# Expert 0's late half, first layer: upper weights against x's two parts side by side

## The chip, the cores and the metric

The kernel runs on one core of one Trainium2 chip. The metric is device time in microseconds (us) of one execution. The kernel before takes 385.37 us (median of 3 runs, 385.09 to 385.86).

## What is computed

A retention layer over 4 sequences of 768 tokens and 8 heads gives 3072 tokens x of 512 features. A gate picks one expert of 8 for each token, and the token's result is the expert's two-layer network, weighted by the gate. Cut to what matters here:

```python
logits = x @ w_gate
expert_idx = np.argmax(logits, axis=1)
...
for e in range(E):
    xe = x[expert_idx == e]
    h = np.maximum(xe @ w1[e], 0.0)      # 512 -> 1024, the first layer
    ye = h @ w2[e]                       # 1024 -> 512, the second layer
    out[expert_idx == e] = gate_w[expert_idx == e, None] * ye
```

The matmuls run on numbers that are rounded to a shorter form (fp32r). To keep fp32's precision, each operand is split into an upper part (the rounded number) and a lower part (what the rounding left), and each product is made of three: upper weights times upper x, lower weights times upper x, upper weights times lower x.

## The kernel before, in words

The retention layer comes first, in 24 chunks of 128 tokens; its rows are scattered by expert into a buffer in HBM. Expert 0's tokens are in two halves: an early one of 192 tokens, whose network runs while the last chunks are still being sent (`early_half`, lines 793 to 841), and a late one of 224 tokens, with which `moe_main` (line 845) begins. The other seven experts follow, at 380 to 452 tokens each.

In `moe_main` the order of the work on each engine is the order of the program, written out by hand (`manual_schedule`, line 986); the framework adds the waits that the data ask for. One pass of the loop over e (line 987) is one expert. Its first layer is a loop over eight blocks f of 128 hidden features (line 1033). For each f:

- TensorE (PE): 12 matmuls into one of three PSUM tiles `ph` (line 1035, taken in turn), 4 blocks of 128 input features for each of the three products (lines 1037 to 1043). The tile must be free: what was read from it three blocks ago must have been read. For expert 0 they have 224 columns.
- ScalarE (ACT): ReLU of `ph` into the upper part `hh` (line 1053). For expert 0 this is two instructions, of 64 and 160 columns, since 64 of the late tokens are put beside the early half's rows.
- VectorE (DVE): the lower part `hl`, ReLU of `ph` minus `hh` (line 1055), for expert 0 again two instructions.
- behind these, on the same queues, the jobs that the program hangs at this f (lines 996 to 1031): for expert 0 at f = 1 two memsets of columns 392 to 451 of `ph0` and `ph1`, at f = 2 a memset of the tile `rare` of the second layer, four small instructions of `token_index` and a memset of the same columns of `ph2`, at f = 3 and f = 4 a part each of the splitting of expert 1's weights (a cast on ACT, line 171, then a subtraction on DVE, line 173), at f = 7 the making of expert 1's x (transposes on DVE, casts on ACT, subtractions on DVE and GpSimd) and two more parts of the splitting. The memsets give columns that a later expert's shorter matmuls leave alone a value.

The second layer of expert 0 follows: two steps of 24 matmuls of 512 columns (line 1094), with a weighting of the rows on DVE (line 949) and one more part of the splitting behind each, then expert 1's first layer, with 12 matmuls of 392 columns for each f. In expert 1 the third block's successor, f = 3, uses the tile that f = 0 used.

Ahead of the loop, x of expert 0's late half is made: a transpose in two pieces (line 705), the upper part by ACT and DVE (lines 707 and 780), the lower part by two subtractions on DVE (lines 781 and 709). Upper and lower part lie in one tile, `xhl1`, of 2 x 4 x 224. Behind the subtractions DVE has some small work (lines 712 to 718) and the weighting of the early half's rows (line 834).

Of the kernel before, what the change touches and what calls it, by code (L numbers as in the profile page):

```python
# [9 lines left out]
F32 = mybir.dt.float32  # L10
# [4 lines left out]
ALU = mybir.AluOpType  # L15
# [5 lines left out]
P = 128  # L21
# [6 lines left out]
EARLY, LATE = 192, 224  # L28
BESIDE = 2 * P - EARLY
# [4 lines left out]
CMAX32 = -(-CMAX // 32) * 32  # L34
E1 = E - 1
E9 = E + 1
KD = DM // P
# [76 lines left out]
def retention_moe(ctx, tc, qkv, wts, cst, gdec, out):  # L114
# [621 lines left out]
    def clear_behind(e, zero):  # L736
        nc.sync.dma_start(out=x_rows[bass.ds(end_at[e], ZROWS), :], in_=zero)

    natural = {0: (sidx0, meta0)}
    moe_main(tc, wparts, fetch, split, leave, one_more, xhl1, hidden_early, third, lim, xgs, clear_behind, load_x, load_meta, token_index, regions, beyond, limit, spare, natural,  # L740
             overflow, out)
    most = nc.values_load(top[0:1, 0:1], min_val=0, max_val=N)  # L742
# [46 lines left out]
def sliver(halves, j):  # L789
    return halves[j // 2][:, j % 2]  # L790
# [54 lines left out]
def moe_main(ctx, tc, wparts, fetch, split, leave, one_more, xhl1, hidden_early, third, lim, xgs, clear_behind, load_x, load_meta, token_index, regions, beyond, limit, spare, natural,  # L845
             overflow, out):
    nc = tc.nc
# [6 lines left out]
    yp = pool("yp", 2)  # L854
# [33 lines left out]
    def by_count(e, products):  # L888

        if e == 0:  # L890
            return products(CAPS[0])
        with tc.If(fewer[e] < 2) as few:
            with tc.If(fewer[e] < 1) as none:
                products(CAPS[e])
            with none.Else():
                products(CAPS[e] - STEPS[e])
        with few.Else():
            with tc.If(fewer[e] < 3) as two:
                products(CAPS[e] - 2 * STEPS[e])
            with two.Else():  # L900
                products(CAPS[e] - 3 * STEPS[e])
# [5 lines left out]
    def after_tile(f):  # L907
        return hs[f][0][0:1, 0:1].bitcast(F32)

    def fetch_behind(e, part, h, of):  # L910
        behind(of)
        fetch(e, part, (h,))

    def rows_behind(e, q, of):
        behind(of)
        load_x(xgs[:, e % 2], regions(e), blocks[e], (q,))
        if q == 3 and e in natural:
            load_meta(meta7[:, 0:len(widths[e])], regions(e), len(widths[e]))
# [67 lines left out]
    with tc.manual_schedule():  # L986
        for e in range(E):
            halves = ((0, nc.vector), (1, nc.vector))
            xh, xl = xs[e]
            cap, nj = CAPS[e], len(widths[e])  # L990
# [42 lines left out]
            for f in range(KF):  # L1033
                fo = (f % 4) * P
                ph = phs[(KF * e + f) % 3]

                def first_layer(w):
                    n = 0
                    for a, x in ((0, xh), (1, xh), (0, xl)):
                        for kd in range(KD):  # L1040
                            nc.tensor.matmul(out=ph[:, :w], lhsT=sliver(wparts[e, f // 4][a], kd)[:, fo:fo + P],  # L1041
                                             rhs=x[:, kd, :w], start=(n == 0), stop=(n == 3 * KD - 1))
                            n += 1

                by_count(e, first_layer)
                hh = hp.tile([P, CMAX], F32R, name="hh", tag="hh", bufs=8)
                hl = hp.tile([P, CMAX], F32R, name="hl", tag="hl", bufs=8)
                parts = [(hh[:, :cap], hl[:, :cap], ph[:, :cap])]
                if e == 0:
                    beside = [t[f][:, EARLY:2 * P] for t in hidden_early]  # L1050
                    parts = [(*beside, ph[:, 0:BESIDE]), (hh[:, :cap - BESIDE], hl[:, :cap - BESIDE], ph[:, BESIDE:cap])]
                for to, low, of in parts:
                    nc.scalar.activation(out=to, in_=of, func=AF.Relu)  # L1053
                for to, low, of in parts:
                    nc.vector.scalar_tensor_tensor(out=low, in0=of, scalar=0.0, in1=to.bitcast(F32),  # L1055
                                                   op0=ALU.max, op1=ALU.subtract)
                hs.append((hh, hl))
                if f % 4 == 3:
                    leave((e, f // 4))
                for fn, a in jobs[f]:  # L1060
                    fn(*a)
                if e == 1 and f == 0:
                    clear_behind(2, zero)
                if more and e:
                    if 2 <= f < 6:
                        rows_behind(e + 1, f - 2, after_tile(f))
                    else:
                        fetch_behind(e + 1, f // 4, f % 2, after_tile(f))
            for k in range(steps):
# [30 lines left out]
                if e == 0 and k == 2:  # L1100
                    with tc.If(fewer[0] > 0) as some:
                        second_layer(cap)
                    with some.Else():
                        nc.tensor.matmul(out=py[:widths[0][2], 0:128], lhsT=hs[0][0][:, P:P + widths[0][2]],
                                         rhs=sliver(wparts[0, 2][0], 0)[:, 0:128], start=True, stop=True)
# [168 lines left out]
```

## Time and profile before

| | |
|---|---|
| median of 3 runs | 385.37 us |
| the profiled execution, its own time | 385.67 us |
| its span, first to last instruction | 383.9 us |
| TensorE matmul busy | 376.5 us, 98% of the span, 3279 matmuls |
| VectorE busy | 259.7 us, 68% |
| ScalarE busy | 154.7 us, 40% |
| GpSimd busy | 166.7 us, 43% |
| granted TensorE clock | 1.000 of full speed |

Times within the trace are in us from the start of the span. PE is the engine's matmuls, PEld its loads of weights. In a timeline each row is a run of like instructions: start, time from the first's start to the last's end, engine, line, operation, output and inputs, form, count, and in brackets how long the engine had been idle and what ended it. Instructions on one engine overlap a little, so a row's start can lie before the end of the row above. The time between the starts of two matmuls that follow one another is called the pitch here; it is less than the duration of one matmul, since they are pipelined.

### The profile page before, as it was taken

What the parts mean: (1) busy time and instruction counts of PE and PEld (TensorE: products, weight loads), DVE (VectorE), ACT (ScalarE), POOL (GpSimd) and SP (SyncE); (2) the same over time, 40 slices, a digit from 0 to 9 for tenths busy, and PEclk for the clock granted to TensorE, in tenths of its full rate; (3) what the DMA queues carried; (4) which work ended last, traced back from release to release, by engine and by line L of the source; (5) the groups of instructions that cost most, each with busy time, mean ns of one, the idle gap of its engine ahead of it and who ended that gap; (6) DMA issues with size and microseconds to landing.
All of it is one profiled execution on the core that took longest, in us unless ns stands there. A gap on an engine that the chain in (4) does not pass through costs nothing. (4 is left out here: it accounts for less than half of the span.)

```text
span 383.9 us, 8981 instructions
## 1 busy us (share of the span) xinstructions
PE 376.5 (98%) x3279; PEld 353.5 (92%) x3279; DVE 259.7 (68%) x571; ACT 154.7 (40%) x315; POOL 166.7 (43%) x149
## 2 busy tenths in 40 slices
PE   8999999999999999999999999999999999999994
PEld 4888888888989899999999999999999999999984
DVE  4647868798888787576665676576747666776511
ACT  3245545544744554334433433253434325443200
POOL 0332544557731221002743385347528444652754
PEclk9999999999999999999999999999999999999999
DMA  7998799998348766555664566366557655761111
GB/s 274 415 372 343 251 404 418 421 388 285 152 106 222 242 211 169 155 189 155 159 207 147 160 170 210 111 175 200 188 151 178 211 187 168 196 197 60 53 47 59
DMA packets 34949, 80.67 MB, mean 210 GB/s; under 512 B 5455, under 2 KB 19411, under 8 KB 32568
## 3 DMA queue, kind: packets, MB, share of 16 engines
q1 hardware_dynamic: 29604, 66.87, 53.8%
q0 software_dynamic: 5264, 12.69, 9.1%
q8 instruction: 58, 0.95, 1.1%
q14 instruction: 19, 0.16, 0.1%
q10 hardware_dynamic: 4, 0.01, 0.0%
HBM read 65.07 MB, written 15.19 MB: 209 GB/s over the span
## 5 line engine op out<-in xcount | busy, mean ns | idle before, releaser
L761 POOL DMA_INDIRECT out<-Z,sidx x82 | 103.9, 1267 | 121.3 <-DVE Z L980 103.8
L173 DVE TENSOR_TENSOR wlo<-raw,whi 128x1024 fp32r<-128x1024 f32 (+1 forms) x72 | 78.7, 1101 | 5.5 <-ACT whi L171 4.7
L171 ACT CAST whi<-raw 128x1024 fp32r<-128x1024 f32 (+1 forms) x72 | 67.0, 953 | 7.5 <-DMA raw<-w 5.6
L1053 ACT ACTIVATE hh<-ph 128x64 fp32r<-128x64 f32 (+7 forms) x72 | 32.3, 460 | 91.5 <-PE ph L1041 91.5
L1096 PE MATMUL py<-hh,wlo 128*128 128x392 f32 (+4 forms) x192 | 66.1, 344 | 0.0
L1096 PE MATMUL py<-hl,whi 128*128 128x392 f32 (+4 forms) x192 | 66.0, 344 | 0.0
L1096 PE MATMUL py<-hh,whi 128*128 128x392 f32 (+4 forms) x192 | 66.0, 344 | 0.0
L1055 DVE SCALAR_TENSOR_TENSOR hl<-ph,hh 128x64 fp32r<-128x64 f32 (+7 forms) x72 | 36.4, 515 | 34.1 <-ACT hh L1053 33.6
L1041 PE MATMUL ph<-xh,wlo 128*128 128x392 f32 (+5 forms) x224 | 49.2, 341 | 0.0
L1041 PE MATMUL ph<-xh,whi 128*128 128x392 f32 (+5 forms) x224 | 49.1, 341 | 0.0
L1041 PE MATMUL ph<-xl,whi 128*128 128x392 f32 (+5 forms) x224 | 48.9, 340 | 0.0
L1041 PEld LDWEIGHTS ph<-xh,whi 128*128 128x128 f32 x224 | 40.3, 189 | 0.3
L1041 PEld LDWEIGHTS ph<-xh,wlo 128*128 128x128 f32 x224 | 40.3, 188 | 0.2
L1041 PEld LDWEIGHTS ph<-xl,whi 128*128 128x128 f32 x224 | 40.3, 188 | 0.2
L274 POOL TENSOR_TENSOR vs<-qkv_t,cs 128x512 f32<-128x512 f32 x19 | 20.4, 1072 | 45.5 <-DMA qkv_t<-qkv 34.2
L1096 PEld LDWEIGHTS py<-hh,wlo 128*128 128x128 f32 x192 | 36.1, 188 | 0.2
L1096 PEld LDWEIGHTS py<-hh,whi 128*128 128x128 f32 x192 | 36.1, 188 | 0.2
L1096 PEld LDWEIGHTS py<-hl,whi 128*128 128x128 f32 x192 | 36.1, 188 | 0.2
L780 ACT CAST xh<-xt 128x512 fp32r<-128x512 f32 (+7 forms) x27 | 14.8, 551 | 48.3 <-DVE xt L771 48.3
L288 DVE TENSOR_TENSOR Sb<-sp,xgs 128x512 f32<-128x512 f32 x48 | 30.0, 683 | 5.3 <-PE sp L285 5.3
L761 POOL DMA_INDIRECT xs_dram<-xn,KEY x24 | 24.9, 1037 | 11.9 <-ACT xn L343 3.4
L975 DVE STREAM_TRANSPOSE Z<-py 128x416 f32<-128x416 f32 (+2 forms) x24 | 15.3, 637 | 20.3 <-PE py L1096 20.0
(168 smaller groups left out, 519.1 us busy)
## 6 DMA issues: line engine op xcount, KB each, us to landing
raw<-w SPq DMA_DIRECT2D x64, 512.0 KB
qkv_t<-qkv SPq DMA_DIRECT2D x18, 1024.0 KB
qkv_t<-qkv SPq DMA_DIRECT2D x4, 768.0 KB
xgs<-xs_dram SPq DMA_DIRECT2D x12, 211.2 KB
qkv_t<-qkv SPq DMA_DIRECT2D x4, 512.0 KB
xgs<-xs_dram SPq DMA_DIRECT2D x8, 227.5 KB
out<-Z,sidx POOLq DMA_INDIRECT x82, 4.1
xs_dram<-zero SPq DMA_DIRECT2D x6, 195.0 KB
```

The costliest lines, as they stand in the source:

```text
L171: nc.scalar.copy(out=to[h][:, a:a + n], in_=raw[:, a:a + n])
L173: engine.tensor_tensor(out=to[h][:, a:a + n], in0=raw[:, a:a + n], in1=parts[0][h][:, a:a + n].bitcast(F32), op=ALU.subtract)
L274: engine.tensor_tensor(out=vs, in0=qs[g][:, 2].rearrange("a (h d) -> a h d", d=D), in1=cv[:, c, :].unsqueeze(2).broadcast_to([P, H, D]), o ...
L288: nc.vector.tensor_tensor(out=Sb[:, r], in0=sps[r], in1=M[:, r], op=ALU.mult)
L761: sc = tc.nc.gpsimd.indirect_dma_start(out=out, out_offset=bass.IndirectOffsetOnAxis(ap=index, axis=0), in_=rows, in_offset=None, bounds_c ...
L780: nc.scalar.copy(out=xh[:, :, sl], in_=src)
L975: nc.vector.transpose(out=Zs[e][:, 0:nb, k, :], in_=py[:, 0:32 * nb].rearrange("p (j c) -> p j c", c=32))
L1041: nc.tensor.matmul(out=ph[:, :w], lhsT=sliver(wparts[e, f // 4][a], kd)[:, fo:fo + P], rhs=x[:, kd, :w], start=(n == 0), stop=(n == 3 * KD ...
L1053: nc.scalar.activation(out=to, in_=of, func=AF.Relu)
L1055: nc.vector.scalar_tensor_tensor(out=low, in0=of, scalar=0.0, in1=to.bitcast(F32), op0=ALU.max, op1=ALU.subtract)
L1096: nc.tensor.matmul(out=py[:, :cols], lhsT=sliver(a, f % 4)[:, k * P:(k + 1) * P], rhs=x[:, :cols], **se)
```

## The change

For expert 0 the first layer is written another way. For each of the 4 blocks of input features one matmul multiplies the upper weights with x's upper and lower parts side by side, into 448 columns of `ph`; 4 matmuls of 224 columns then add the lower weights times the upper x to the first 224 columns. So 8 matmuls stand in the place of 12. Behind them ACT copies columns 224 to 447 to a slice of its own in an SBUF tile (a `Z` tile of the pool `yp`, which the result rows of expert 1 used first before), DVE adds columns 0 to 223 to it in place, and ReLU and subtraction read that sum in place of `ph`. All other experts keep the old form. The memsets of `ph` stay where they were.

```diff
@@ -1034,6 +1034,15 @@
                 fo = (f % 4) * P
                 ph = phs[(KF * e + f) % 3]
 
+                def beside_layer():
+                    both = ph[:, 0:2 * LATE]
+                    for a in range(2):
+                        for kd in range(KD):
+                            nc.tensor.matmul(out=ph[:, 0:LATE] if a else both.rearrange("p (s c) -> p s c", s=2),
+                                             lhsT=sliver(wparts[e, f // 4][a], kd)[:, fo:fo + P],
+                                             rhs=xh[:, kd] if a else xhl1[:, :, kd], start=(not a and kd == 0),
+                                             stop=(a == 1 and kd == KD - 1), skip_group_check=True)
+
                 def first_layer(w):
                     n = 0
                     for a, x in ((0, xh), (1, xh), (0, xl)):
@@ -1042,13 +1051,21 @@
                                              rhs=x[:, kd, :w], start=(n == 0), stop=(n == 3 * KD - 1))
                             n += 1
 
-                by_count(e, first_layer)
+                if e:
+                    by_count(e, first_layer)
+                else:
+                    beside_layer()
+                    if f == 0:
+                        sums = yp.tile([P, CMAX32 // 32, KD, 32], F32, name="Z").rearrange("p j k r -> p (j k r)")
+                    both = sums[:, f * LATE:(f + 1) * LATE]
+                    nc.scalar.copy(out=both, in_=ph[:, LATE:2 * LATE])
+                    nc.vector.tensor_tensor(out=both, in0=ph[:, 0:LATE], in1=both, op=ALU.add)
                 hh = hp.tile([P, CMAX], F32R, name="hh", tag="hh", bufs=8)
                 hl = hp.tile([P, CMAX], F32R, name="hl", tag="hl", bufs=8)
                 parts = [(hh[:, :cap], hl[:, :cap], ph[:, :cap])]
                 if e == 0:
                     beside = [t[f][:, EARLY:2 * P] for t in hidden_early]
-                    parts = [(*beside, ph[:, 0:BESIDE]), (hh[:, :cap - BESIDE], hl[:, :cap - BESIDE], ph[:, BESIDE:cap])]
+                    parts = [(*beside, both[:, 0:BESIDE]), (hh[:, :cap - BESIDE], hl[:, :cap - BESIDE], both[:, BESIDE:cap])]
                 for to, low, of in parts:
                     nc.scalar.activation(out=to, in_=of, func=AF.Relu)
                 for to, low, of in parts:
```

## Rows read from the trace of the kernel before

**Rows 1.** Busy time by stretch: busy us of each engine (instructions), PE clock, DMA, GB/s

```profile
115.10:126.06 10.96, 10.96 (x98) 10.92 (x97) 9.12 (x35) 4.77 (x16) 1.00 (x1) 1.00 0.93 224
126.06:137.10 11.04, 11.04 (x50) 8.94 (x49) 8.51 (x12) 5.79 (x10) 3.02 (x3) 1.00 0.77 256
137.10:376.00 238.90, 238.90 (x1323) 235.47 (x1322) 156.07 (x294) 90.03 (x130) 109.54 (x87) 1.00 0.54 160
```

**Rows 2.** Timeline of PE: expert 0's late first layer, start of its second

```profile
115.12 0.67 PE L1041 MATMUL ph<-xhl,whi 128*128 128x224 f32 x4
...
116.10 1.15 PE L1041 MATMUL ph<-xhl,whi 128*128 128x224 f32 x8
117.09 0.61 PE L1041 MATMUL ph<-xhl,wlo 128*128 128x224 f32 x4
...
118.43 0.61 PE L1041 MATMUL ph<-xhl,wlo 128*128 128x224 f32 x4
...
119.81 0.61 PE L1041 MATMUL ph<-xhl,wlo 128*128 128x224 f32 x4
...
126.06 0.40 PE L1094 MATMUL py<-whi,hh 128*128 128x512 f32 x1
```

**Rows 3.** Timeline of PE: two blocks of the early half, 192 columns

```profile
105.99 0.61 PE L812 MATMUL ph<-xhl,wlo 128*128 128x192 f32 x4
...
107.33 0.61 PE L812 MATMUL ph<-xhl,wlo 128*128 128x192 f32 x4
```

**Rows 4.** Timeline of PE: expert 1's first layer, f = 0 and f = 3

```profile
137.10 0.22 PE L1104 MATMUL between<-whi,hh 128*32 128x128 f32 x1
137.16 0.92 PE L1041 MATMUL ph<-xh,whi 128*128 128x392 f32 x4
...
143.60 0.86 PE L1041 MATMUL ph<-xh,whi 128*128 128x392 f32 x4
```

**Rows 5.** Timeline of DVE: x's lower part, the first blocks, the memsets

```profile
115.49 0.55 DVE L709 TENSOR_TENSOR xhl<-xt,xhl 128x384 fp32r<-128x384 f32 x1
...
117.17 0.75 DVE L834 TENSOR_SCALAR xn<-py,meta 128x512 f32<-128x512 f32 x1
...
118.63 0.46 DVE L1055 SCALAR_TENSOR_TENSOR hl<-ph,hh 128x64 fp32r<-128x64 f32 x2 [0.35 <-ACT hh L1053]
119.10 0.18 DVE L1061 MEMSET ph<- 128x60 f32 x2
...
120.52 0.48 DVE L1061 MEMSET between<- 32x512 f32 x1
...
121.59 0.11 DVE L1061 MEMSET ph<- 128x60 f32 x1
```

**Rows 6.** Groups by form on ACT, 115 to 142: busy us, mean ns, idle before

```profile
L171 ACT CAST whi<-raw 128x1024 fp32r<-128x1024 f32 x7 | 7.1, 1048 | 1.9 <-DVE wlo L173 1.9
L1053 ACT ACTIVATE hh<-ph 128x160 fp32r<-128x160 f32 x8 | 2.4, 299 | 0.0
...
L1053 ACT ACTIVATE hh<-ph 128x440 fp32r<-128x440 f32 x2 | 1.1, 540 | 2.4 <-PE ph L1041 2.4
```

**Rows 7.** Timeline of ACT: a block's ReLUs, expert 1's x, casts of its weights

```profile
118.18 0.42 ACT L1053 ACTIVATE hh<-ph 128x64 fp32r<-128x64 f32 x2 [0.92 <-PE ph L1041]
...
127.82 1.22 ACT L780 CAST xh<-xt 128x512 fp32r<-128x512 f32 x2 [1.14 <-DVE xt L771]
...
135.75 2.00 ACT L171 CAST whi<-raw 128x1024 fp32r<-128x1024 f32 x2 [1.93 <-DVE wlo L173]
```

**Rows 8.** Groups by form on DVE, 114 to 142

```profile
L173 DVE TENSOR_TENSOR wlo<-raw,whi 128x1024 fp32r<-128x1024 f32 x7 | 8.5, 1220 | 1.2 <-ACT whi L171 1.1
L1055 DVE SCALAR_TENSOR_TENSOR hl<-ph,hh 128x160 fp32r<-128x160 f32 x8 | 2.5, 307 | 0.0
```

**Rows 9.** Timeline of DVE: behind expert 0's last block, ahead of expert 1's first

```profile
127.08 1.29 DVE L771 STREAM_TRANSPOSE xt<-xgs 128x512 f32<-128x512 f32 x2
...
138.64 1.21 DVE L173 TENSOR_TENSOR wlo<-raw,whi 128x1024 fp32r<-128x1024 f32 x1
```

## The prediction

> **What bounds the kernel now.** I first read busy time by stretch. In expert 0's late first layer, in its second layer and from there to 376 us, matmuls fill every stretch at the full granted clock [rows 1]. So PE is the path: what the late first layer gains or loses moves every later matmul by as much, unless a wait further down takes it. DVE is busy 9.12 of 10.96 us in that layer and 8.51 of 11.04 in the next stretch, ACT 4.77 and 5.79 [rows 1]. DVE has some 2 us to give, and the change puts eight instructions more on it. So I then read the timelines of PE, DVE and ACT there, for order and hand-overs.
>
> **PE's own saving.** A block f now takes 1.34 us (117.09 to 118.43) for 12 matmuls, a pitch of 0.112 us [rows 2]. Blocks of 192 columns also take 1.34 us [rows 3], so at 224 columns the pitch isn't set by columns: something that each matmul pays once does it, and four fewer matmuls save time. For 448 columns I go between two rows: 392 columns have 0.179 us (36 matmuls from 137.16 to 143.60 [rows 4]) and 512 have 0.230 (48 from 126.06 [rows 2] to 137.10 [rows 4]); 448 gives 0.203. A block then takes 4 x 0.203 + 4 x 0.112 = 1.26 us, 0.084 less; eight save 0.67 us. Bounds: 0.179 (1.4 us saved) and 0.224, two matmuls of 224 (nothing saved). I keep 0.203, since the two widths lie close.
>
> Weighed against it: the rows show equal pitch at 192 and 224 columns [rows 2, 3]. The Trainium skill, "TensorE: Matmul & The Clock Gate", section "Back-to-back issue gap", gives the gap of an isolated matmul as its columns at one per cycle plus some 2.5 ns; by that eight blocks would save 32 x 2.5 ns, an estimate of 0.08 us, and the change's gain would be gone. The equal pitch speaks against that rule here.
>
> **Edit 1: the first matmul needs x's lower part.** Today that part enters with a block's third group, at 116.10 [rows 2]; now the first matmul reads it. The last subtraction runs from 115.49 to 116.04 [rows 5]. From DVE's end to PE I take 0.13 to 0.15 us: the first of two memsets ends about 119.21 [rows 5], and block 3, which uses that tile, begins at 119.81 - 4 x 0.112 = 119.36 [rows 2], 0.04 late by the even beat. So block 0 begins at 116.17 in place of 115.12: 1.05 us lost. Today's block 0 lasts 0.18 us longer than the others (115.12 to 117.09 - 0.45 = 116.64 [rows 2]); that goes.
>
> **Edit 2: a loop between ACT and DVE.** Today a block's chain is ReLU, then subtraction, and both engines wait for PE. Now it is copy (ACT), add (DVE), ReLUs (ACT), subtractions (DVE), and both queues keep program order. Durations: the copy, 224 columns out of PSUM, lies between ReLUs of 160 and 440 columns (0.299 and 0.540 us [rows 6]), on their line 0.35. The add lies between the subtraction of 160 (0.307 [rows 8]) and that of 384 columns (0.55 [rows 5]), 0.38. The two ReLUs take 0.42 [rows 7], the two subtractions 0.46 [rows 5], some 0.42 to the next start when queued. ACT to DVE takes 0.03 us (118.18 + 0.42 to 118.63 [rows 5, 7]), DVE to ACT under 0.1 (two transposes take 1.29 us from 127.08 [rows 9], so the first ends about 127.73; ACT starts at 127.82 [rows 7]), taken as 0.05. From add to add: 0.38 + 0.05 + 0.42 + 0.03 + 0.42 = 1.30 us. The copy of the next block hides under the subtractions. So DVE needs 1.30 us where PE needs 1.26, before any other job on DVE.
>
> **Edit 2 with its jobs, in order.** Block 0's matmuls end at 117.42; ACT starts 0.2 later (today 118.18 [rows 7] behind 117.98), copy to 117.97, add(0) at 118.01: DVE is just through with the weighting that starts at 117.17 [rows 5]. add(1) at 119.31, its subtractions end near 120.61, the memsets of `ph0` and `ph1` by 120.79. These memsets write columns 392 to 451, which today's matmuls don't touch; the new ones write to 447, so the order is now due to the data too. Block 3 waits for `ph0`: 120.77 + 0.15 = 120.92, where PE would be ready at 119.93: 0.98 us. add(2) at 120.79, subtractions to 122.09; then `rare`, indices and the third memset, 1.07 us from 120.52 to 121.59 [rows 5], so add(3) at 123.29. Block 5, free behind that memset, loses 0.02. ACT's cast of 1.05 us [rows 6] comes behind ReLU(3), from 124.02, DVE's cut, 1.22 [rows 8], at 125.10; add(4) only at 126.25. Block 7 uses the tile of block 4: add(4) ends at 126.63, plus 0.15 is 126.78; PE is ready at 125.96, 0.82 us lost. Block 7 ends at 128.03, today 126.06 [rows 2]: PE is **1.97 us** late. As a sum: 1.05 - 0.18 + 0.98 + 0.02 + 0.82 - 0.67 = 2.02, less rounding. The second layer takes the hidden features in order, three matmuls or 0.69 us for each: the last upper part is due at 128.03 + 7 x 0.69 = 132.9, its lower part 0.46 later. ReLU(7) ends at 132.7, the subtraction at 132.9: just in time.
>
> **What is late next.** The second cast and cut put add(5) at 129.21; add(6) 130.51, add(7) 131.81; DVE reaches expert 1's x at 133.1, today at 127.08 [rows 9]: **6.0 us** late, while PE is 2.0 late. Behind it DVE has hardly a pause until its cut at 138.64, ending 139.85 [rows 9]; where it pauses it waits for ACT, and ACT's casts at 135.75 wait for DVE's cut [rows 7], so the pauses move along. The cut now ends near 145.8, expert 1's first subtraction (0.62 us, an estimate on the line of rows 5 and 8) near 146.4. Expert 1's f = 3 uses that tile: 146.4 + 0.15 = 146.5, today 143.60 [rows 4]; PE by its own lateness would be there at 145.6. So 0.9 us more: **+2.9 us** in all. Further waits I don't see: from there on DVE is idle for a third of the time, 156.07 us busy of 238.90 [rows 1].
>
> Edits at nothing: the sum's slices are one per block, so no write waits for an old reader; expert 1's result rows move to the pool's other buffer, needed only in its second layer. SP's fetches follow PE's freed weights and shift by 1 to 2 us; casts that need them shift by more. GpSimd gets nothing new.
>
> **Sum.** 385.67 (the profiled run's own time: span 383.9 plus 1.8 around it) + 2.9 = 388.6; the median of the runs shown lies 0.3 lower: **388.3 us**. Unknown costs: with copy and add at their lower ends the chain gives +2.3, at their upper ends +4.5; the bounds of 448 columns move it by 0.1 either way.
>
> **Rivals.**
> - *The backlog is caught up.* If DVE's and ACT's pauses between 127 and 140 shrink by about 1 us, expert 1's f = 3 doesn't wait, and only the first layer's lengthening stays: +1.97, 387.3 us (1.6 to 2.2 by the bounds). For it: DVE is idle 2.5 of 11.04 us there [rows 1]. Against: its pauses are waits for ACT, which waits for DVE [rows 7]. Chance 0.27.
> - *The chain keeps pace.* If copy, add and hand-overs overlap more than I think, so that add to add is under 1.26 us less its jobs, blocks 3 and 7 don't wait; block 0's wait stays: 1.05 - 0.18 - 0.67 = +0.2, 385.6 us. Against: the order on both queues is fixed, and DVE's time in the layer would be 9.12 + 8 x 0.38 = 12.2 us against 10.1 for PE. Chance 0.06.
> - *Faster.* The mechanism is PE's pitch in the late first layer: saving at its upper bound, 1.4 us, and both the wait for the lower part and the loop hidden. It decides from a block's consumers taking less than PE's 1.26 us, with the lower part ready by 115.1. Time 383.9 to 384.7. Against: the subtraction's end at 116.04 [rows 5] is a fact of today. Chance 0.07, 0.02 of that within 0.2%.
> - *The 448 columns run like two matmuls of 224*, so that the change doesn't do what it says: nothing saved, the DVE chain sets the end all the same, +3.0. It lies within the forecast.
>
> **How the numbers follow.** Forecast 0.60, of 387.7 to 389.8. The range, 386.6 to 389.7, holds forecast and first rival but for their tails, some 0.8. About 0.2%, 0.77 us, is what a measurement here can tell from no change. Slower: 0.60 + 0.27 = 0.87; within: 0.06 + 0.02 = 0.08; faster 0.05.
>
> **What would show it.** In the timeline of PE: first 448-column matmul near 116.2; gaps ahead of blocks 3 and 7 and of expert 1's f = 3; second layer from 128.0. A block without a wait lasts 1.26 us; 1.34 would deny the saving. On DVE: adds 1.30 us apart where no job lies between, expert 1's first transpose near 133. The prediction is wrong if block 3 begins on the beat, or if the second layer starts before 126.1.

## The result, and the profile after

The kernel after takes 387.98 us (median of 5 runs, 387.68 to 388.19), beside 385.37 for the kernel before (5 runs, 385.09 to 386.33): a ratio of 1.0061, 95% interval 1.005 to 1.0072. It is slower by 2.6 us. The forecast was 388.3, its range 386.6 to 389.7.

The profiled execution took 388.19 us, its span is 386.4. First the page's line of busy time:

```profile
PE 376.8 (98%) x3247; PEld 352.5 (91%) x3247; DVE 262.9 (68%) x579; ACT 157.4 (41%) x323; POOL 166.7 (43%) x149
```

32 matmuls fewer (8 blocks, 4 each), and PE's busy time is what it was. DVE has 3.2 us more, ACT 2.7. Next the busy time by stretch, cut as [rows 1], but for the first stretch, which begins here with the early half's last matmul, some 0.3 us ahead of where [rows 1] begins:

```profile
114.89:127.92 13.03, 11.07 (x67) 9.84 (x65) 9.79 (x36) 5.85 (x18) 1.00 (x1) 1.00 0.94 252
127.92:138.99 11.07, 11.07 (x51) 8.94 (x49) 8.70 (x17) 5.79 (x16) 2.58 (x2) 1.00 0.66 212
139.00:376.00 237.00, 236.63 (x1302) 232.89 (x1301) 157.80 (x296) 91.61 (x132) 108.67 (x85) 1.00 0.53 159
```

In each the clock that the throttle granted is 1.00, TensorE's full speed. Expert 0's late first layer is no longer full: PE is busy 11.07 of 13.03 us. The second layer is full, and behind 139 there is one gap, of 0.37 us (237.00 less 236.63). All PE waits between 115 and 376 us are these four (waiting instruction, releaser, us in total, times, longest):

```profile
PE ph L1041 <- DVE xhl L709: 0.9, 1, 0.9
PE ph L1041 <- DVE ph L1078: 0.7, 1, 0.7
PE ph L1041 <- DVE Z L1062: 0.4, 1, 0.4
PE ph L1050 <- DVE hl L1072: 0.4, 1, 0.4
```

That is the order of the forecast: x's lower part, the memset of `ph0`, an add, and expert 1's first subtraction. Where they lie, in the timeline of PE:

```profile
116.14 1.06 PE L1041 MATMUL ph<-xhl,whi 128*128 128x448 f32 x4 [0.86 <-DVE xhl L709]
...
117.47 1.00 PE L1041 MATMUL ph<-xhl,whi 128*128 128x448 f32 x4
118.30 0.60 PE L1041 MATMUL ph<-xhl,wlo 128*128 128x224 f32 x4
118.74 0.99 PE L1041 MATMUL ph<-xhl,whi 128*128 128x448 f32 x4
...
120.85 1.06 PE L1041 MATMUL ph<-xhl,whi 128*128 128x448 f32 x4 [0.69 <-DVE ph L1078]
...
122.19 0.99 PE L1041 MATMUL ph<-xhl,whi 128*128 128x448 f32 x4
...
124.72 0.99 PE L1041 MATMUL ph<-xhl,whi 128*128 128x448 f32 x4
...
126.55 1.09 PE L1041 MATMUL ph<-xhl,whi 128*128 128x448 f32 x4 [0.40 <-DVE Z L1062]
...
127.92 0.40 PE L1111 MATMUL py<-whi,hh 128*128 128x512 f32 x1
...
146.02 0.98 PE L1050 MATMUL ph<-xh,whi 128*128 128x392 f32 x4 [0.37 <-DVE hl L1072]
```

PE is 1.86 us late at the second layer (126.06 in [rows 2]) and 2.42 at expert 1's f = 3 (143.60 in [rows 4]). The timeline of DVE shows what they wait for:

```profile
118.05 0.39 DVE L1062 TENSOR_TENSOR Z<-ph,Z 128x224 f32<-128x224 f32 x1 [0.18 <-ACT Z L1061]
118.76 0.55 DVE L1072 SCALAR_TENSOR_TENSOR hl<-Z,hh 128x64 fp32r<-128x64 f32 x2 [0.32 <-ACT hh L1070]
119.32 0.39 DVE L1062 TENSOR_TENSOR Z<-ph,Z 128x224 f32<-128x224 f32 x1
...
120.60 0.17 DVE L1078 MEMSET ph<- 128x60 f32 x2
120.68 0.38 DVE L1062 TENSOR_TENSOR Z<-ph,Z 128x224 f32<-128x224 f32 x1
...
123.06 0.42 DVE L1062 TENSOR_TENSOR Z<-ph,Z 128x224 f32<-128x224 f32 x1
...
124.97 1.23 DVE L173 TENSOR_TENSOR wlo<-raw,whi 128x1024 fp32r<-128x1024 f32 x1 [0.62 <-ACT whi L171]
126.11 0.38 DVE L1062 TENSOR_TENSOR Z<-ph,Z 128x224 f32<-128x224 f32 x1
...
129.13 0.38 DVE L1062 TENSOR_TENSOR Z<-ph,Z 128x224 f32<-128x224 f32 x1
...
132.66 1.30 DVE L771 STREAM_TRANSPOSE xt<-xgs 128x512 f32<-128x512 f32 x2
...
145.36 0.61 DVE L1072 SCALAR_TENSOR_TENSOR hl<-ph,hh 128x440 fp32r<-128x440 f32 x1
```

The adds are 1.27 us apart where nothing lies between (118.05 to 119.32), 2.38 with the jobs of f = 2, and 3.05 and 3.02 with a cut of expert 1's weights. Expert 1's transposes begin 5.58 us later than today's 127.08 [rows 9], and its first subtraction, at 145.36, is what PE waits for at f = 3. The ReLU which that subtraction reads had ended by 143.77 in ACT's timeline: from there on it is DVE's own queue that holds it up.

### The profile page after: what moved, and what is told of

Read it like the earlier page. It is cut to its first block, busy times and chain, and to the rows that moved or that the text cites. A ratio compares the mean times of both kernels' runs of the same rounds, so it can differ in the third digit from the quotient of the medians.

```text
span 386.4 us, 8924 instructions
## 1 busy us (share of the span) xinstructions
PE 376.8 (98%) x3247; PEld 352.5 (91%) x3247; DVE 262.9 (68%) x579; ACT 157.4 (41%) x323; POOL 166.7 (43%) x149
## 5 line engine op out<-in xcount | busy, mean ns | idle before, releaser
L1070 ACT ACTIVATE hh<-ph 128x440 fp32r<-128x440 f32 (+6 forms) x56 | 29.0, 518 | 81.6 <-PE ph L1050 81.6
L1072 DVE SCALAR_TENSOR_TENSOR hl<-ph,hh 128x440 fp32r<-128x440 f32 (+6 forms) x56 | 32.9, 587 | 30.6 <-ACT hh L1070 30.1
```

## The experiments

Six kernels undo or move one part of the change, two put several together, one takes the copy and the add out with the order turned, one makes a single edit to the kernel before, and both kernels ran once more.

All of these runs but after_again were on chips on which even the kernel before takes 393.4 to 393.5 us. The excess lies in the retention layer, where in all their profiles the granted clock is at half speed (1.2 GHz) for a stretch that begins between 94 and 97 us, behind waits of PE (from 88 to 95 us it is busy 4.1 to 5.5 us, in the three other profiles all 7.0); by 103 us it is back at full speed (2.4 GHz). That excess is scattered by more than the effects looked for: in these profiles the stage defined next begins anywhere between 121.08 and 124.09 us.

So the main measure is **the stage**: from the start of the last subtraction for x's lower part (line 709) to the first matmul of expert 1's f = 3. It doesn't depend on when the retention layer ends. "The rest" goes from there to the last weighting's start (line 966). The first four expectations speak of the whole run, since the stage was chosen only after those four kernels had run.

| kernel | stage, us | rest, us | whole run against before, ratio and 95% interval |
|---|---|---|---|
| before | 28.11 | 235.31 | |
| before, again | 28.11 | 235.30 | 1.0 (0.9979 to 1.002) |
| after | 30.58 | 235.43 | 1.0061 (1.005 to 1.0072) |
| after, again | 30.57 | 235.46 | 1.0055 (1.0034 to 1.0076) |
| memsets_late | 30.69 | 235.44 | 1.0084 (1.0059 to 1.0108) |
| low_weights_first | 30.20 | 237.99 | 1.0089 (1.0059 to 1.012) |
| twelve_narrow | 30.52 | 235.46 | 1.008 (1.0056 to 1.0104) |
| no_add | 28.58 | 237.25 | 1.0019 (0.9997 to 1.0041) |
| no_add_low_first | 27.95 | 236.41 | 1.0009 (0.9983 to 1.0036) |
| pool_cut_early | 30.50 | 235.43 | 1.0104 (1.0049 to 1.0158) |
| combined | 30.27 | 235.60 | 1.0078 (1.0047 to 1.0109) |
| second_split_late | 30.05 | 235.41 | 1.0114 (1.0088 to 1.014) |
| combined2 | 27.93 | 235.97 | 1.0017 (0.9992 to 1.0043) |
| before_pool_cut | 28.11 | 235.31 | a single run |

The stage repeats to 0.01 us for both kernels, and after less before is +2.47 in it and +0.12 in the rest. In low_weights_first and no_add the rest is about 2 us longer; the trace shows PE waits there, all in a second layer with matmuls of 366 columns near 350 us (1.5 us for a lower x part and 0.5 for nothing that the profile names in the one, 1.4 for nothing it names in the other). no_add_low_first and combined2 have 0.7 and 0.3 us of the kind at the same place. Why was not followed up, and no reading below uses the rest of these four.

The ratios of the whole run don't follow the stage everywhere: second_split_late has the largest, 1.0114, and a shorter stage than the kernel after. Only one execution of each kernel has a profile, and that of second_split_late was the shortest of its four; where the other three lost their time isn't known. So the whole run says of the versions that none is shown to be faster than the kernel before, and no more.

Two theories stood against each other. **Sum:** PE's losses add up, so a wait taken away, or a saving of PE given up, moves the end by its own size. **Chain:** the order of DVE's and ACT's queues sets the end, and PE's waits only show it; one taken away comes back at the next place.

**The two kernels again.** Before: 

> The kernel before once more, for the spread of the stage time between chips: 28.1 us within 0.15 us, whatever the whole run takes.

After: 

> The changed kernel once more, for the spread of its stage time between chips: 30.6 us within 0.15 us, and 235.4 us from expert 1's f = 3 to the last weighting, as in its first profile, whatever the whole run takes.

The times are in the table: the result and the stage both repeat.

**The memsets later.** They stay the same three, but behind f = 6, 7 and 5:

```diff
-                    job(1 + i // 2, nc.vector.memset, phs[i][:, CAPS[1] - 3 * STEPS[1]:], 0.0)
+                    job((6, 7, 5)[i], nc.vector.memset, phs[i][:, CAPS[1] - 3 * STEPS[1]:], 0.0)
```

> Chain theory (the loop of ACT and DVE and DVE's backlog set when expert 1's f = 3 may begin): block 3 begins on the beat near 120.0 in place of 120.85, but block 7 then waits longer, some 1.2 us, and DVE is at best 0.2 to 0.3 us earlier; the time falls by 0.1 to 0.3 us against the changed kernel, to about 387.8. Sum theory (each wait of PE is paid on its own): the 0.69 us wait before block 3 is gone from the end, 387.3 us or less.

PE's waits in this stage:

```profile
PE ph L1041 <- DVE Z L1062: 1.1, 1, 1.1
PE ph L1041 <- DVE xhl L709: 0.8, 1, 0.8
PE ph L1050 <- DVE hl L1072: 0.7, 1, 0.7
```

The wait for the memset is gone and block 3 is on the beat; but block 7 now waits 1.13 us where it waited 0.40, and expert 1's f = 3 0.71 where it waited 0.37. The stage is 0.11 longer, not 0.69 shorter. Sum falls here. Chain had the direction of the waits right and expected a small gain that didn't come; 0.11 us more is not explained.

**Lower weights first.** The 4 matmuls of 224 columns, which don't need x's lower part, go ahead of the 4 of 448:

```diff
-                    for a in range(2):
+                    for a in (1, 0):
...
-                                             rhs=xh[:, kd] if a else xhl1[:, :, kd], start=(not a and kd == 0),
-                                             stop=(a == 1 and kd == KD - 1), skip_group_check=True)
+                                             rhs=xh[:, kd] if a else xhl1[:, :, kd], start=(a == 1 and kd == 0),
+                                             stop=(not a and kd == KD - 1), skip_group_check=True)
```

> Lower weights first, so that x's lower part is needed only by the fifth matmul. Chain theory: block 0 begins near 115.2 in place of 116.14, the first add comes only 0.27 us earlier, since DVE is busy until 117.8 with the weighting; block 3 waits some 1.6 us for the memset; the end comes 0.2 to 0.3 us earlier, 387.7 us. Sum theory: the 0.86 us wait comes back in full, 387.1 us.

The wait for x's lower part drops from 0.86 to 0.30 us, the three others stay at 0.8, 0.4 and 0.4, and the stage is 0.38 shorter (0.27 if it is counted from the early half's last matmul). So much of edit 1 was real loss, less than its 0.86. For block 3 the expectation had 1.6 us of waiting, twice what came.

**Twelve narrow.** Each matmul of 448 columns is cut in two of 224, everything behind them stays, so PE's saving is given up:

```diff
...
+                            for x, to in ((xh, 0), (xl, LATE))[:2 - a]:
+                                nc.tensor.matmul(out=ph[:, to:to + LATE],
+                                                 lhsT=sliver(wparts[e, f // 4][a], kd)[:, fo:fo + P],
+                                                 rhs=x[:, kd], start=(not a and not to and kd == 0),
+                                                 stop=(a == 1 and kd == KD - 1), skip_group_check=True)
```

> Each matmul of 448 columns cut in two of 224, all else as changed, the same sums. Chain theory: a block lasts 1.34 us in place of 1.27, blocks 3 and 7 wait less, expert 1's f = 3 begins within 0.1 us of where it does in the changed kernel: 388.0 us, no difference. Sum theory: the 0.57 us that the wide matmuls save are lost, 388.55 us.

In its timeline of PE two blocks that follow one another begin 1.34 us apart:

```profile
124.50 1.05 PE L1041 MATMUL ph<-xhl,whi 128*128 128x224 f32 x8
...
125.84 1.05 PE L1041 MATMUL ph<-xhl,whi 128*128 128x224 f32 x8
```

PE's work is 0.07 us longer per block, 0.56 in all, and the stage isn't longer at all (30.52). Block 7's wait is no longer listed, and expert 1's is 0.30. What the wide matmuls save was spent waiting.

**Without copy and add.** ReLU and subtraction read `ph[:, 0:LATE]`. This leaves out the product of upper weights with lower x in expert 0's late half.

```diff
-                    nc.scalar.copy(out=both, in_=ph[:, LATE:2 * LATE])
-                    nc.vector.tensor_tensor(out=both, in0=ph[:, 0:LATE], in1=both, op=ALU.add)
+                    both = ph[:, 0:LATE]
```

> Copy and add left out and ReLU and subtraction read the first 224 columns of the PSUM tile, so that the product of upper weights and lower x is left out of expert 0's late half. Chain theory: only block 0's wait and the pitch are left, 0.86 + some 0.1 - 0.57: PE reaches the second layer near 126.4, no wait in expert 1: 385.7 us, 0.3 us over the kernel before. Sum theory of PE's four waits: the same waits for the memset stay if they are a matter of the wider tile and not of the loop, 386.4 us.

One wait is left in the stage:

```profile
PE ph L1041 <- DVE xhl L709: 1.0, 1, 1.0
```

The stage is 28.58. So 2.00 of the 2.47 us come with copy and add (and with ReLU and subtraction reading the sum from SBUF), and the other 0.47 is edit 1 less PE's saving.

**The same, lower weights first and memsets late** (the diffs of the three kernels above together):

> No copy and no add, the lower weights first and the memsets late; the product of upper weights and lower x is left out of expert 0's late half. What the wide matmuls save by themselves: no wait of PE is left, a block lasts 1.27 us in place of 1.34, stage time 28.1 - 0.57 = 27.5 us, 0.5 to 0.6 us under the kernel before run beside it. Rival (the isolated gap of a matmul goes by its columns): a block keeps its time, stage time 28.1.

27.95, a miss: 0.16 below before, not 0.6. The fifth matmul still waits 0.30 us for x's lower part. That bounds the change: with the sum free of charge, these matmuls in this place gain 0.16 us.

**Expert 1's first cuts on GpSimd**, so that DVE is relieved of the two cuts at f = 3 and f = 4:

```diff
-                        job(s0 + i * (s0 < KF - 1), split, e + 1, part, i, eng)
+                        job(s0 + i * (s0 < KF - 1), split, e + 1, part, i, nc.gpsimd if part == 0 else eng)
```

> The two subtractions of expert 1's first weights, hung at f = 3 and f = 4, on GpSimd in place of DVE; ACT's casts stay where they are. Stage time is from the start of the last subtraction for x's lower part to the first matmul of expert 1's f = 3: 28.1 us before, 30.6 changed. Chain theory (DVE's backlog sets both late waits): DVE is some 1.7 us earlier at expert 1's first transpose, PE waits neither for block 7 nor for expert 1's f = 3, stage time 29.4 to 29.6. Rival (the waits come from the order on ACT, whose casts hold up the copies): the casts stay, so both waits stay, stage time 30.6.

30.50, a clear miss, and the trace has the reason. First GpSimd's timeline, then DVE's:

```profile
133.18 4.98 POOL L173 TENSOR_TENSOR wlo<-raw,whi 128x1024 fp32r<-128x1024 f32 x2 [5.89 <-ACT whi L171]
```

```profile
133.36 0.39 DVE L1062 TENSOR_TENSOR Z<-ph,Z 128x224 f32<-128x224 f32 x1 [0.85 <-ACT Z L1061]
134.08 1.81 DVE L1072 SCALAR_TENSOR_TENSOR hl<-Z,hh 128x64 fp32r<-128x64 f32 x2 [0.32 <-ACT hh L1070]
135.81 0.38 DVE L1062 TENSOR_TENSOR Z<-ph,Z 128x224 f32<-128x224 f32 x1
136.52 1.96 DVE L1072 SCALAR_TENSOR_TENSOR hl<-Z,hh 128x64 fp32r<-128x64 f32 x2 [0.32 <-ACT hh L1070]
```

While GpSimd cuts, DVE's pair of subtractions lasts 1.81 and 1.96 us; it takes 0.55 elsewhere. Both inputs of such a subtraction lie in SBUF now (`Z` and `hh`). The adds, with one operand in PSUM, keep their 0.38. DVE reaches expert 1's transposes 17.16 us after the stage began, after 17.22 in the kernel after: it won nothing. PE no longer waits for block 7, but 0.8 us in place of 0.4 at expert 1's f = 3. Two rivals for this remain, GpSimd's work as such and the place of the operands. The next run but one tells them apart.

**All moves together**: lower weights first, memsets late, the memset of `rare` and the indices at f = 6, the first cuts on GpSimd at f = 5 and 6, and two of expert 0's weightings on ACT:

```diff
-                job(2, nc.vector.memset, rare[0:widths[0][2]], 0.0)
-                job(2, token_index, sidx0[:, 1:4], meta0[:, 1:4], lim[:, 1:4], "joint")
+                job(6, nc.vector.memset, rare[0:widths[0][2]], 0.0)
+                job(6, token_index, sidx0[:, 1:4], meta0[:, 1:4], lim[:, 1:4], "joint")
...
+                        job(5 + i if part == 0 else s0, split, e + 1, part, i, nc.gpsimd if part == 0 else eng)
```

> The change with lower weights first, the memsets behind the last use of each tile, the early memset of the second layer's tile and the index work at f = 6, expert 1's first splitting at f = 5 and 6 with the subtractions on GpSimd, and the weighting of two row blocks on ACT in place of DVE. Chain theory: nothing holds up blocks 3 and 7, DVE reaches expert 1's x some 2 us late and has 1.5 us less behind it, so expert 1's f = 3 does not wait: stage time 27.5 to 27.7 us, 0.4 to 0.6 us under the kernel before run beside it. Sum of the parts as rival (some other job now waits, the copies behind ACT's casts at f = 6 above all): no better than before, stage time 28.1 or more.

30.27, a miss from the same cause. PE waits nowhere behind block 0 of expert 0's first layer, but 1.3 us in the second layer for the last ReLU and 0.6 at expert 1's f = 3. Even an index instruction of three columns is held up. GpSimd's timeline, then DVE's:

```profile
132.83 4.97 POOL L173 TENSOR_TENSOR wlo<-raw,whi 128x1024 fp32r<-128x1024 f32 x2 [6.69 <-ACT whi L171]
```

```profile
133.73 1.81 DVE L1075 SCALAR_TENSOR_TENSOR hl<-Z,hh 128x64 fp32r<-128x64 f32 x2 [0.32 <-ACT hh L1073]
...
136.05 1.77 DVE L226 TENSOR_TENSOR far<-cs,lim 128x3 f32<-128x3 f32 x1
```

It ends at 137.82 us, GpSimd's second cut at 137.80: it is held until GpSimd is through.

**The kernel before with its first cuts on GpSimd.** The same edit as in pool_cut_early, but there the subtraction reads `ph` in PSUM.

> The kernel before, with the two subtractions of expert 1's first weights on GpSimd. In the changed kernel that stretched DVE's subtractions to as much as 1.5 us each. If it hits only instructions that read both operands from SBUF, the subtractions here, with one operand in PSUM, keep 0.46 us a pair and stage time stays at 28.1. If it hits every instruction of DVE, a pair takes 1.8 us as there.

GpSimd's timeline, then DVE's:

```profile
129.64 4.87 POOL L173 TENSOR_TENSOR wlo<-raw,whi 128x1024 fp32r<-128x1024 f32 x2 [3.14 <-ACT whi L171]
```

```profile
129.99 0.46 DVE L1055 SCALAR_TENSOR_TENSOR hl<-ph,hh 128x64 fp32r<-128x64 f32 x2 [0.70 <-ACT hh L1053]
131.33 0.46 DVE L1055 SCALAR_TENSOR_TENSOR hl<-ph,hh 128x64 fp32r<-128x64 f32 x2 [0.88 <-ACT hh L1053]
```

The pairs keep their 0.46 us under GpSimd's cuts, and the stage its 28.11. It is the place of the operands, not GpSimd's work as such.

**The second split later.** Expert 1's weight splitting that hangs at expert 0's second layer (two cuts) goes to expert 1's f = 0 and 1, and what was there to f = 6 and 7. Nothing of expert 0's first layer changes:

```diff
-                    job(i + int(e > 1), split, e, 3, i, eng)
+                    job(i + 1 if e > 1 else i + 6, split, e, 3, i, eng)
+                    if e == 1:
+                        job(i, split, e, 2, i, eng)
...
-                if more and e == 0 and k < 2:
-                    split(e + 1, 2, *halves[k])
```

> The changed kernel, with the splitting of the third quarter of expert 1's weights moved from expert 0's second layer to expert 1's f = 0 and 1, and that of the last quarter to f = 6 and 7: DVE has 2.4 us less ahead of expert 1's first subtraction. Theory (DVE's backlog makes expert 1's f = 3 wait): that wait of 0.37 us and the restart behind it go, the waits in expert 0 stay, stage time 30.0 to 30.1 us in place of 30.6. Rival (that wait has another cause): stage time 30.6.

The three waits of expert 0 stay, the fourth is gone, and the stage is 30.05, as expected:

```profile
PE ph L1043 <- DVE xhl L709: 0.8, 1, 0.8
PE ph L1043 <- DVE ph L1080: 0.7, 1, 0.7
PE ph L1043 <- DVE Z L1064: 0.4, 1, 0.4
```

So it was DVE's backlog behind expert 0, queued ahead of expert 1's first subtraction, that cost the last 0.53 us.

**The moves without GpSimd**: lower weights first, memsets late, `rare` and indices at f = 6, the first cuts at f = 7 on their own engines, and the second split later. All its edits stand in the diffs above but one:

```diff
-                        job(s0 + i * (s0 < KF - 1), split, e + 1, part, i, eng)
+                        job(KF - 1, split, e + 1, part, i, eng)
```

> Lower weights first, memsets behind the last use of each tile, the second layer's memset and the index work at f = 6, expert 1's first splitting at f = 7 on ACT and DVE, the later splittings as in the run beside it; nothing on GpSimd. Theory (jobs on the two queues, not the loop itself, make PE wait): no wait but 0.3 us for x's lower part, stage time 27.9 to 28.0 us, 0.1 to 0.3 us under the kernel before: not to be told from it by the whole run. Rival (the loop alone holds PE up even without jobs): block 7 waits, stage time 28.5 or more.

27.93, as expected. One wait is left in the stage, and the blocks lie on the beat. DVE's timeline at the stage's start, then PE's, the first blocks and the second layer's start:

```profile
122.43 0.55 DVE L709 TENSOR_TENSOR xhl<-xt,xhl 128x384 fp32r<-128x384 f32 x1
```

```profile
122.11 0.64 PE L1043 MATMUL ph<-xhl,wlo 128*128 128x224 f32 x4
123.04 1.08 PE L1043 MATMUL ph<-xhl,whi 128*128 128x448 f32 x4 [0.30 <-DVE xhl L709]
123.97 0.60 PE L1043 MATMUL ph<-xhl,wlo 128*128 128x224 f32 x4
...
132.84 0.40 PE L1113 MATMUL py<-whi,hh 128*128 128x512 f32 x1
```

Copy and add are all there, and from the stage's start to the second layer it takes 10.41 us (122.43 to 132.84) where before takes 10.57 (115.49 [rows 5] to 126.06 [rows 2]). So the loop between ACT and DVE alone holds PE up nowhere; it does so with the other jobs of the two queues between its passes. The stage is 0.18 below before's, but the whole run, at 1.0017 (0.9992 to 1.0043), can't be told from before's. No version here is shown to beat the kernel before.

## Why the prediction was right

The likeliest case came, with a size a little too large: +2.6 where +2.9 was forecast.

- **What bounds the kernel.** Right. Where PE was held up, all later matmuls moved with it: the last weighting starts at 381.45 in place of 378.91, 2.54 later, and the rest is only 0.12 longer.
- **PE's saving.** A block takes 1.27 us (117.47 to 118.74), not 1.26: a pitch of 0.207 for 448 columns (0.83 us from 117.47 to 118.30, by 4), between the two rows where it was put. 0.56 us saved, not 0.67. That none of the 0.56 reaches the end is what twelve_narrow shows. By the formula for an isolated matmul in the Trainium skill, "TensorE: Matmul & The Clock Gate", section "Back-to-back issue gap", some 0.08 us would have been saved, an estimate. The section says itself that in a stream of matmuls with their weight loads the formula counts too little at small widths, and the measured 0.56 bears that out.
- **Edit 1.** The first block begins at 116.14 (forecast 116.17). Its loss in the sum was put at 1.05 less 0.18. Turning the order gives back 0.3 to 0.4 of it, and 0.63 where copy and add are left out (28.58 to 27.95): behind a queue that sets the end the rest wasn't there to be won. The 0.18 didn't go in full either, for the block behind the wait lasts 1.33 us (116.14 to 117.47).
- **Edit 2, the hand-overs.** Copy 0.34 and add 0.39 us by the groups below, where 0.35 and 0.38 were taken. The two ReLUs take 0.48 from SBUF, not 0.42, the two subtractions 0.55, not 0.46. Yet add to add is 1.27 us where PE sets the pace and 1.17 to 1.18 where the passes are queued (combined2), not 1.30. What the sum had missed is overlap: in the first pass DVE's first subtraction starts at 118.76, before ACT's pair of ReLUs (0.48 from 118.47 in ACT's timeline) is through.

The groups by form on ACT and DVE, from 115 to 147 us:

```profile
L1061 ACT COPY Z<-ph 128x224 f32<-128x224 f32 x8 | 2.7, 339 | 3.9 <-PE ph L1041 3.9
L1070 ACT ACTIVATE hh<-Z 128x160 fp32r<-128x160 f32 x8 | 2.6, 321 | 0.0
```

```profile
L1062 DVE TENSOR_TENSOR Z<-ph,Z 128x224 f32<-128x224 f32 x8 | 3.1, 389 | 0.2 <-ACT Z L1061 0.2
L1072 DVE SCALAR_TENSOR_TENSOR hl<-Z,hh 128x160 fp32r<-128x160 f32 x8 | 2.6, 326 | 0.0
```

- **The jobs in order.** Block 3 at 120.85 (forecast 120.92), block 7 at 126.55 (126.78), the second layer at 127.92 (128.03): each releaser as named. The term that was too long is the pass of 1.30: six passes are 0.03 to 0.13 shorter than forecast, two with a cut 0.06 and 0.09 longer (3.02 and 3.05, not 2.96), and by the end of the layer that makes the 0.4 us by which DVE's transposes come earlier (132.66, not 133.1). PE's losses ahead of blocks 0, 3 and 7 are 1.02 (against today's 115.12), 0.84 and 0.56 (against the beat of 1.27), where 1.05, 0.98 and 0.82 were put. On the other side the three blocks behind a wait last 1.33, 1.34 and 1.37 us, 0.23 more in all, which no term has, and less was saved. These errors offset one another, so that the sum came within 0.1 us (1.86, forecast 1.97) is in part luck.
- **What is late next.** Right in kind: expert 1's f = 3 waits for its first subtraction, at 146.02 (forecast 146.5), the same 0.4 to 0.5 earlier. second_split_late takes that wait away and nothing else, so the backlog is shown. The step from +1.86 to +2.42 is the 0.9 of the forecast, measured at 0.56: the largest of the differences, and most of why the forecast is too high.
- **The rivals.** *The backlog is caught up* would have been +1.97; DVE's work in the next stretch didn't shrink (8.70 us, 8.51 in [rows 1]). *The chain keeps pace* had its place right, and combined2 shows its condition: not a shorter loop but the jobs moved from between its first passes. *Faster* has its bound in no_add_low_first. *Like two matmuls of 224* is refuted by the block of 1.27, and its guess that this would not matter is borne out.
- **The argument's weak point.** The forecast added up PE's losses, and came out right because it followed DVE's queue for each of them. Read as prices of parts, those terms are wrong: taking away the memsets' wait, priced at 0.98, gave nothing. Only the last wait, which has none behind it, gave back what it measured: 0.53 in second_split_late.

Left open: the longer rest of four versions, the whole-run ratio of second_split_late, and whether an earlier lower part of x, which was not tried, would make the change pay; by no_add_low_first and combined2 the 0.30 us of waiting is what it could add.

## What to carry to other kernels

Fewer matmuls save PE time only if what drains them keeps pace: count, on the queues of ACT and DVE, all that stands between two passes of the new loop, and follow it past the edited layer to the next tile that PE needs. When several waits follow one another on PE, ask whether one queue makes them all; then none but the last has a price of its own, and it takes moving the jobs, not the waits. Moving an operand from PSUM to SBUF can also change whom an instruction collides with.

## What was unexpected of the hardware

A GpSimd instruction that reads SBUF holds up a DVE instruction with both operands in SBUF, and not one with an operand in PSUM: 1.81 to 1.96 us in place of 0.55 for a pair of subtractions, and 0.46 unchanged with `ph` as an operand. The Trainium skill, "SBUF — State Buffer", section "Who interferes with whom", says so of a DVE instruction with two SBUF inputs beside a GpSimd instruction that reads SBUF; the traces agree, and the expectations of pool_cut_early and combined had overlooked it. The hold lasts until GpSimd's instruction ends, and GpSimd's cuts themselves take 4.97 and 4.98 us for two, where they take 4.87 beside subtractions with an operand in PSUM. It can be read in both kernels as well, where DVE and GpSimd each make a part of expert 1's lower x, in the timelines of DVE and of GpSimd for the kernel after:

```profile
137.54 1.31 DVE L781 TENSOR_TENSOR xl<-xt,xh 128x224 fp32r<-128x224 f32 x1 [0.64 <-ACT xh L780]
```

```profile
137.31 1.30 POOL L781 TENSOR_TENSOR xl<-xt,xh 128x512 fp32r<-128x512 f32 x1 [1.91 <-ACT xh L780]
```

DVE's 224 columns last 1.31 us and end 0.24 us behind GpSimd's 512, while 384 columns take 0.55 us when DVE is alone [rows 5]. GpSimd also needs some 2.45 us for a cut of 1024 columns (4.87 for two) that takes DVE 1.22 [rows 8].
